# A recurrent attention and mixture-of-experts kernel: the first two units' gate sums spread by one-hot products

## The chip, the cores and the metric

The kernel runs on one core of one Trainium2 chip. The metric is the device time of one execution in microseconds. The core's engines are named as in the profile: PE (TensorE, PEld its weight loads), DVE (VectorE), ACT (ScalarE), POOL (GpSimd) and SP (SyncE, which here only issues DMAs).

## The reference

Two layers follow each other. The first is a gated linear recurrence over 768 time steps for 4 batches of 8 heads with 40 columns each. Its log-space gates are stabilised by a running maximum:

```
m_new = max(f[t] + m, i[t]);  fs = exp(f[t] + m - m_new);  is = exp(i[t] - m_new)
C = fs*C + is * outer(v[t], k[t]);   n = fs*n + is*k[t]
y[t] = sigmoid(o[t]) * (C @ q[t]) / max(|n . q[t]|, 1)
```

The second takes the 3072 rows of 320 columns, picks two of eight experts for each by noisy logits, and adds the two weighted expert outputs, relu(x @ w1[e]) @ w2[e] with 1024 hidden columns.

## The kernel before

The recurrence is worked off in chunks of 64 steps. A *unit* is one chunk of two batches (16 heads, kept as two halves p of 8 heads), and there are 24 units: two pairs of batches by 12 chunks. The state of a pair goes from chunk to chunk inside the buffer of keys and values.

For unit u the steps are: `s_part` (line 326), products of keys and queries on PE into PSUM; `e_part` (305), one matmul for each half that puts the logarithm of the decay matrix into PSUM, and ACT's exponential of it into W; `k_part` (340), DVE scales the keys by W's last column (kd); `p_part` (346), DVE multiplies scores and W; `c_part` (355), PE builds the new state (st) and ACT copies it into the next unit's buffer; `o_part` (368), PE's output products; `f_part` (374), DVE normalises them (dn, tm) and POOL multiplies by the sigmoid gate SG, which gives the row tile XR; `keep_rows` (386) stores XR to memory from POOL's queue; `t_part` (393), PE transposes XR for the router's logits.

The matmul of `e_part` multiplies LE by RE. LE holds, for two units at a time, an identity in rows 0 to 63, the sums a(t) of each head (high and low halves, 32 rows) in rows 64 to 95, and ones in rows 96 and 97. RE holds the causal mask in rows 0 to 63, a one-hot choice of the head in rows 64 to 95, and in rows 96 and 97 the sums g(t) of all heads side by side. There are two LE and two RE, used in turn by pairs of units. Their fixed parts are written by `operands` (223) and `heads` (230).

`gate_math` (189) makes both sums for 128 time steps of all heads on DVE: eight operations, of which the first (192) needs the gate data `fit` and the last (211) writes HL, in 64 rows (head and half) by time. `gate_move` (216) then carries 128 columns of HL to LE and RE with two DMAs, since the sums of 32 rows have to stand side by side in two rows. The first two moves are issued from SP, the third from POOL between units 0 and 1, the others from POOL at even units.

Before the loop, in the order of the program: the gate data of 128 steps, the constants `cet`, keys and queries of unit 0 in four DMAs (rows 0 to 31 and 32 to 39 of each half), an identity, gate data of steps 128 to 383, values of unit 0 (lines 173 to 183); rows that the loads don't fill are written with zeros by `blank` (169) on DVE and POOL. ACT fills LE[0], issues unit 1's four key loads, and fills RE[0] (245 to 252). DVE does the gate math of steps 0 to 127, then that of 128 to 255 (260). `keys` (239) writes zeros and identities into the value buffers on POOL. `gate_steps(4)` (269) does half of the third gate math; its other half, and the rest, are spread over the loop (829, 854). PE warms up with products of zeros (`warm`, 681), 16 of them, does the scores of unit 0, 12 more, and then unit 0's `e_part` (686 to 694).

The loop (785) does for each i, in this order on each engine's own queue: loads of unit i+3, `keep_rows(i-1)`, `k_part` and `p_part` of unit i+1, `c_part` and `o_part` of unit i, the first half of `e_part(i+2)`, `f_part(i)`, gate steps, `t_part(i-1)`, `s_part(i+2)`, the second half of `e_part(i+2)`. Every engine and every DMA queue works in the program's order. DMAs of SP and ACT use eight completion semaphores in turn, so that a DMA waits for the eighth before it to have landed. W, p and kd have two buffers, the output products' PSUM tile one.

From unit 6 on the first expert's weights are loaded and split, from unit 7 on tokens are routed; after the loop the experts are worked off. None of this is touched.

Of the kernel before, what the change touches and what calls it, by code (L numbers as in the profile page):

```python
# [18 lines left out]
L = 64  # L19
# [21 lines left out]
WARM, WARM2 = 16, 12  # L41
# [13 lines left out]
E_H, E_L, E_P, E_SG, E_END = 64, 72, 264, 266, 268  # L55
# [6 lines left out]
def build(ctx, tc, qk, vk, fi, noise, wgn, w1, w2, cst, ce, out):  # L62
# [84 lines left out]
    def load_unit(u, what="kv", q=None):  # L147
        pr, c = divmod(u, NCH)
        if "k" in what:
            for n in (slice(0, 32), slice(32, D)):  # L150
                for p in range(2):
                    (q or SP).dma_start(QK[u % 4][64 * p + n.start:64 * p + n.stop], qk[pr, c, p, n])
        if "v" in what:
            flat = VKS[u % 4].rearrange("p x c -> p (x c)")
            SP.dma_start(flat[0:64, 0:VW], vk[pr, c, 0])
            SP.dma_start(flat[64:128, 648:648 + VW], vk[pr, c, 1])
# [4 lines left out]
    cet = raw[0:KE, 2 * S:2 * S + E_END]  # L161
# [7 lines left out]
    def blank(i, q):  # L169
        q.memset(QK[i][32:64], 0.0)  # L170
        q.memset(QK[i][96:128], 0.0)

    SP.dma_start(fit[:, :, 0:128], fi[:, :, 0:128])
    SP.dma_start(cet, ce)
    V.memset(mt[:, 0:1], -1e30)
    blank(0, V)
    blank(1, P)
    V.memset(rmt[:, 0:256], 1.0)
    V.memset(rmt[:, 0:256].rearrange("p (c t) -> p c t", t=L)[:, :, 0], 0.0)
    load_unit(0, "k")  # L180
    SP.dma_start(cs[:, 0:128], cst[:, 0:128])
    SP.dma_start(fit[:, :, 128:384], fi[:, :, 128:384])
    load_unit(0, "v")

# [31 lines left out]
    def gate_move(kk, q=(SP, SP)):  # L216
        pr, k = divmod(kk, GB)
        j = kk % 2
        src = HL[32 * pr:32 * pr + 32, :, k * GC * L:(k + 1) * GC * L].bitcast(F32)
        q[0].dma_start(LE[j][64:96, :, 64:128].bitcast(F32), src[:, 0].rearrange("r (c t) -> r c t", c=GC))  # L220
        q[1].dma_start(RE[j][96:98].bitcast(F32), src[:, 1])

    def operands(j, p, eng=None):
        if p is None:
            A.activation(LE[j][0:KE], cet[0:KE, None, E_L:E_L + 192].to_broadcast([KE, GC, 192]), AF.Copy)
        else:
            A.activation(RE[j][0:64, p].rearrange("r h (c t) -> r h c t", c=GC),
                         cet[0:64, None, None, 0:L].to_broadcast([64, H, GC, L]), AF.Copy)

    def heads(j, p, eng):  # L230
        o, i = RE[j][64:96, p], cet[64:96, E_H:E_H + H, None].to_broadcast([32, H, GC * L])
        x = cet[64:96, E_P + p:E_P + p + 1]
        if eng is A:
            A.activation(o, i, AF.Copy, scale=x)
        else:
            V.tensor_scalar(o, i, x, None, op0=OP.mult)
# [8 lines left out]
    operands(0, None, A)  # L245
    load_unit(1, "k", A)
    run(gate_math(0, GC * L))
    gate_move(0)
    operands(0, 0, A)
    operands(0, 1, A)  # L250
    heads(0, 0, A)
    heads(0, 1, A)
    load_unit(1, "v")
    blank(2, P)
    for i in range(2):
        keys(i)
    load_unit(2, "k")
    operands(1, None, A)
    operands(1, 0, A)
    run(gate_math(GC * L, 256))  # L260
    gate_move(1)
    heads(1, 0, V)
# [6 lines left out]
    gate_steps(4)  # L269
    blank(3, P)  # L270
    for i in range(2, 4):
        keys(i)
    load_unit(2, "v")
    load_unit(3, "k")
    SP.dma_start(fit[:, :, 384:], fi[:, :, 384:])
# [29 lines left out]
    def e_part(u, ps_=(0, 1), first=False):  # L305
        pr, c = divmod(u, NCH)
        j = (GB * pr + c // GC) % 2
        c = c % GC
        for p in ps_:
            ps = XTB if first and p else psum.tile([128, 512], F32, name="e")  # L310
            T.matmul(ps, LE[j][0:KE, c, 64 - 64 * p:192 - 64 * p], RE[j][0:KE, p, :, c * L:c * L + L], start=True, stop=True)  # L311
            if p == 0:
                W[u] = wk.tile([128, 2, H, L], F32, name="w", bufs=LEAD)
            A.activation(W[u][:, p].rearrange("p h t -> p (h t)"), ps, AF.Exp)
# [31 lines left out]
    def p_part(u):  # L346
        PP[u] = wk.tile([128, 2, H, L], F32, name="p")
        if whole(u):
            V.tensor_mul(PP[u], SQ[u], W[u])
        else:  # L350
            for p in range(2):
                n = half[p]
                V.tensor_mul(PP[u][n, p], SQ[u][n, p], W[u][n, p])
# [20 lines left out]
    def f_part(u, step):  # L374
# [8 lines left out]
        V.scalar_tensor_tensor(tm, dn[:, :, None].to_broadcast([128, H, D]), 1.0, ps[:, :, 0:D], op0=OP.min, op1=OP.mult)  # L383
        P.tensor_mul(XR[u], tm.rearrange("p h d -> p (h d)"), SG[u % 4])  # L384
# [306 lines left out]
    e_part(0, first=True)  # L691
    s_part(1)
    heads(1, 1, A)
    e_part(1, first=True)
    operands(1, 1, A)
    k_part(0)
    p_part(0)
# [86 lines left out]
    i = 0  # L784
    while i < NU - LEAD:
# [42 lines left out]
        f_part(i, lambda: fill(0.15, False))  # L828
        if i < 2:
            gate_steps(4)  # L830
        if i == 0:
            gate_move(2, (P, P))
# [429 lines left out]
def consts():  # L1262
# [16 lines left out]
    e = np.zeros((KE, E_END), np.float32)  # L1279
# [3 lines left out]
    e[96:98, E_L:E_L + 192] = 1  # L1283
# [7 lines left out]
    return c, e  # L1291


def layout(i):
# [27 lines left out]
    c, e = consts()  # L1322
    return dict(qk=qk, vk=vk, fi=fi, noise=nz, wgn=wgn, w1=w1, w2=w2, cst=c, ce=e)
# [20 lines left out]
```

## Time and profile before

| what | us |
|---|---|
| median of 3 runs (526.47 to 527.35) | 526.8 |
| the profiled execution's own time | 524.22 |
| its span, from the first to the last instruction | 522.0 |
| PE busy | 499.3 |
| DVE busy | 339.4 |
| ACT busy | 248.3 |
| POOL busy | 235.7 |

The span is what the views of the trace cover; 2.2 us of the execution lie around it. Times in the trace count from the start of the span. A busy engine is not one at its peak: PE's records overlap. The chain of waits follows the work that ended last back to its start, and names at each step what released it. Its pieces marked "issue" are time in which an engine waited for nothing that the profile shows.

### The profile page before, as it was taken

How to read it: one execution, taken by the hardware profiler on the slowest of the kernel's cores; microseconds unless marked ns; L12 is line 12 of the kernel's file. 1: busy time of each engine (PE TensorE's matmuls, PEld its weight loads, DVE VectorE, ACT ScalarE, POOL GpSimd, SP SyncE). 2: the span in 40 equal slices, each digit the busy share in tenths (PEclk: the TensorE clock that was granted, in tenths of full speed). 3: DMA queues.
4: the chain of work that ended last, by engine and by line, in shares of the span. 5: the costliest groups of instructions: out<-in, count | busy, mean ns of one | idle time of the engine just before them, and what ended most of it. 6: DMA issues, size and time to landing. Idle time of an engine off the chain costs nothing.

```text
span 522.0 us, 13295 instructions
## 1 busy us (share of the span) xinstructions
PE 499.3 (96%) x5129; PEld 469.8 (90%) x5130; DVE 339.4 (65%) x913; ACT 248.3 (48%) x594; POOL 235.7 (45%) x313
## 2 busy tenths in 40 slices
PE   7899989999999899999999999999999999999993
PEld 3788878878989788999999999999999999999993
DVE  7999997986978376763765485367548357555310
ACT  5978978868532255432533354054325315515300
POOL 7545776863324836045415623460562254151033
PEclk9999999999999899999999999999999999999998
DMA  5899999885766627068229515832951583272033
GB/s 155 194 252 240 243 257 237 231 203 199 238 200 213 135 36 222 1 126 264 79 46 274 115 29 128 240 91 46 253 105 52 113 248 88 62 167 26 2 40 40
DMA packets 39737, 76.87 MB, mean 147 GB/s; under 512 B 10389, under 2 KB 29532, under 8 KB 37876
## 3 DMA queue, kind: packets, MB, share of 16 engines
q1 hardware_dynamic: 27636, 52.19, 35.4%
q0 software_dynamic: 11616, 20.57, 20.5%
q10 hardware_dynamic: 416, 3.21, 1.7%
q8 instruction: 42, 0.69, 0.6%
q14 instruction: 27, 0.22, 0.1%
HBM read 52.42 MB, written 17.40 MB: 134 GB/s over the span
## 4 chain that ended last, share of the span: by engine, by line
PE 63%; DVE 13%; DMA 12%; issue 5%; ACT 4%; POOL 2%; SPq 0%; POOLq 0%; DVEq 0%; ACTq 0%
PE s L973 14%; DMA y_out<-y,tok 9%; PE e L973 8%; PE st L1001 4%; PE st L1000 4%; PE o L1001 4%; PE st L999 4%; PE o L1000 4%; PE o L999 4%; PE o L372 3%; PE e L311 2%; DVE hlo L985 2%; PE st L363 2%; PE s L335 2%; PE xt L415 2%
## 5 line engine op out<-in xcount | busy, mean ns | idle before, releaser
L1027 POOL DMA_INDIRECT y_out<-y,tok x53 | 86.9, 1640 | 188.0 <-DVE y L1017 184.9
L984 ACT ACTIVATE hh<-s 128x384 fp32r<-128x384 f32 (+3 forms) x91 | 42.6, 470 | 82.8 <-PE s L973 78.8
L973 PE MATMUL s<-xh,w1h 128*128 128x384 f32 (+6 forms) x273 | 76.5, 335 | 0.0
L743 POOL DMA_INDIRECT xg<-rows,tok x53 | 57.3, 1082 | 29.0 <-issue 15.9
L985 DVE SCALAR_TENSOR_TENSOR hlo<-s,hh 128x384 fp32r<-128x384 f32 (+3 forms) x91 | 47.5, 523 | 22.3 <-ACT hh L984 19.5
L973 PE MATMUL s<-xh,w1l 128*128 128x384 f32 (+6 forms) x273 | 61.7, 334 | 0.0
L1001 PE MATMUL o<-w2h,hlo 128*128 128x320 f32 x184 | 56.9, 309 | 0.7 <-DVE hlo L985 0.7
L1000 PE MATMUL o<-w2l,hh 128*128 128x320 f32 x184 | 56.8, 309 | 0.0
L999 PE MATMUL o<-w2h,hh 128*128 128x320 f32 x184 | 56.3, 306 | 0.2 <-ACT hh L984 0.2
L1001 PE MATMUL st<-w2h,hlo 128*128 128x320 f32 x168 | 52.5, 312 | 0.0
L1000 PE MATMUL st<-w2l,hh 128*128 128x320 f32 x168 | 52.5, 312 | 0.0
L999 PE MATMUL st<-w2h,hh 128*128 128x320 f32 x168 | 51.9, 309 | 0.0
L973 PEld LDWEIGHTS s<-xh,w1h 128*128 128x128 f32 x273 | 49.2, 188 | 1.1
L973 PEld LDWEIGHTS s<-xh,w1l 128*128 128x128 f32 x273 | 47.7, 188 | 1.1 <-DVE xh L777 0.2
L973 PE MATMUL s<-xl,w1h 128*128 128x384 f32 (+6 forms) x182 | 46.0, 334 | 0.0
L984 ACT ACTIVATE hh<-e 128x384 fp32r<-128x384 f32 (+3 forms) x45 | 21.3, 473 | 50.3 <-PE e L973 49.2
L973 PE MATMUL e<-xh,w1h 128*128 128x384 f32 (+6 forms) x135 | 38.8, 341 | 1.1 <-DVE hlo L985 0.6
L1017 DVE TENSOR_SCALAR y<-st,gw 128x320 f32<-128x320 f32 x20 | 11.0, 551 | 43.0 <-PE st L1001 37.1
L1017 DVE TENSOR_SCALAR y<-o,gw 128x320 f32<-128x320 f32 x22 | 12.1, 550 | 39.4 <-PE o L1001 39.3
L384 POOL TENSOR_TENSOR xr<-tm,vk 128x320 f32<-128x320 f32 x24 | 20.9, 873 | 33.9 <-DMA qk<-qk_in 6.8
L1001 PEld LDWEIGHTS o<-w2h,hlo 128*128 128x128 f32 x184 | 34.5, 187 | 0.9 <-DVE hlo L985 0.9
L999 PEld LDWEIGHTS o<-w2h,hh 128*128 128x128 f32 x184 | 34.5, 188 | 0.7 <-ACT hh L984 0.5
(236 smaller groups left out, 1271.8 us busy)
## 6 DMA issues: line engine op xcount, KB each, us to landing
vk<-vk_in SPq DMA_DIRECT2D x48, 242.0 KB
raw<-w_in SPq DMA_DIRECT2D x6, 1536.0 KB
raw<-w_in SPq DMA_DIRECT2D x6, 1280.0 KB
qk<-qk_in SPq DMA_DIRECT2D x46, 128.0 KB
y_out<-zrow SPq DMA_DIRECT2D x15, 320.0 KB
rows<-xr POOLq DMA_DIRECT2D x23, 160.0 KB
xt__2799<-xb SPq DMA_DIRECT2D x40, 72.0 KB
xt__2799<-xb SPq DMA_DIRECT2D x40, 48.0 KB
```

Source lines behind the costliest of these rows:

```text
L311: T.matmul(ps, LE[j][0:KE, c, 64 - 64 * p:192 - 64 * p], RE[j][0:KE, p, :, c * L:c * L + L], start=True, stop=True)
L372: T.matmul(OQ[u][half[p], h, :], PP[u][n, p, h, :], VK[u % 4][p][n, h * 41:h * 41 + 41], start=True, stop=True)
L384: P.tensor_mul(XR[u], tm.rearrange("p h d -> p (h d)"), SG[u % 4])
L743: P.indirect_dma_start(out=XG[0:rows_of(e, t), t], out_offset=None, in_=XD[0:n], in_offset=bass.IndirectOffsetOnAxis(ap=token(e, t), axis= ...
L973: T.matmul(ps[:, 0:n], l, r, start=i == 0, stop=i == len(ops) - 1)
L984: A.activation(hi, x, AF.Relu)
L985: V.scalar_tensor_tensor(lo, x, 0.0, hi.bitcast(F32), op0=OP.max, op1=OP.subtract)
L999: T.matmul(ps, HH[:, j, c], W2H[:, j], start=j == 0, stop=False)
L1000: T.matmul(ps, HH[:, j, c], W2L[:, j], start=False, stop=False)
L1001: T.matmul(ps, HLO[:, j, c], W2H[:, j], start=False, stop=j == 7)
L1017: V.tensor_scalar(y[0:n], ps[0:n], GW[e][0:n, t:t + 1], None, op0=OP.mult)
L1027: st = P.indirect_dma_start(out=out, out_offset=bass.IndirectOffsetOnAxis(ap=token(e, t), axis=0), in_=y[0:n], in_offset=None, compute_op= ...
```

## The change

For units 0 and 1 the sums g no longer go to RE by DMA. RE[0] gets 32 rows (96 to 127) in place of two, LE[0] ones in rows 96 to 127, and `spread` multiplies the 32 rows of HL, repeated over the heads, by a one-hot table: on DVE for unit 0, on POOL for unit 1. The matmul of `e_part` for these units goes over 128 rows. The sums a of the first three pairs of units go into LE by a copy on DVE; g of the second and third pair still by DMA. The gate math of the first 256 steps is done at once, with 256 steps of gate data in the first load, and the rest of the gate data is loaded later, behind unit 2's keys. Units 0 and 1 load keys in two DMAs of 40 rows; unit 1's are issued from SP. The blanks of units 0 and 1 are on POOL, those of unit 2 on DVE and ACT. The one-hot choice of heads in RE[1] is loaded by a DMA of POOL from a new input, `hd` (32 rows of 2048 numbers). Fewer warming products are made. `p_part(0)` is done half by half around `k_part(0)`; the first half of the third gate math stands before the loop, its second half, the third move and `keys(3)` inside `f_part(0)`, between tm and POOL's product XR.

```diff
-WARM, WARM2 = 16, 12
+WARM, WARM2 = 11, 6
...
-            for n in (slice(0, 32), slice(32, D)):
+            for n in (slice(0, 32), slice(32, D)) if u > 1 else (slice(0, D),):
...
-    cet = raw[0:KE, 2 * S:2 * S + E_END]
+    cet = raw[:, 2 * S:2 * S + E_END]
...
-    SP.dma_start(fit[:, :, 0:128], fi[:, :, 0:128])
+    SP.dma_start(fit[:, :, 0:256], fi[:, :, 0:256])
     SP.dma_start(cet, ce)
     V.memset(mt[:, 0:1], -1e30)
-    blank(0, V)
-    blank(1, P)
+    for i in range(2):
+        blank(i, P)
+    A.activation(QK[2][96:128], wz[96:128, None, None, 0:L].to_broadcast([32, 2, H, L]), AF.Copy)
     V.memset(rmt[:, 0:256], 1.0)
     V.memset(rmt[:, 0:256].rearrange("p (c t) -> p c t", t=L)[:, :, 0], 0.0)
+    V.memset(QK[2][32:64], 0.0)
     load_unit(0, "k")
     SP.dma_start(cs[:, 0:128], cst[:, 0:128])
-    SP.dma_start(fit[:, :, 128:384], fi[:, :, 128:384])
     load_unit(0, "v")
+    load_unit(1)
...
-        q[0].dma_start(LE[j][64:96, :, 64:128].bitcast(F32), src[:, 0].rearrange("r (c t) -> r c t", c=GC))
-        q[1].dma_start(RE[j][96:98].bitcast(F32), src[:, 1])
+        le = LE[j][64:96, :, 64:128], src[:, 0].rearrange("r (c t) -> r c t", c=GC)
+        if kk < 3:
+            V.tensor_copy(*le)
+        else:
+            q[0].dma_start(le[0].bitcast(F32), le[1])
+        if kk:
+            q[1].dma_start(RE[j][96:98].bitcast(F32), src[:, 1])
+
+    def spread(c, p, q):
+        t = slice(c * L, c * L + L)
+        q.tensor_mul(RE[0][96:128, p, :, t], HL[0:32, None, 1, t].bitcast(F32).to_broadcast([32, H, L]),
+                     cet[0:32, E_Q + 8 * p:E_Q + 8 * p + H, None].to_broadcast([32, H, L]))
...
+        if p is None:
+            P.dma_start(RE[j][64:96], hd.bitcast(FR))
+            return
...
-    operands(0, None, A)
-    load_unit(1, "k", A)
-    run(gate_math(0, GC * L))
+    heads(1)
+    keys(0)
+    operands(0)
+    for c in range(GC):
+        for p in range(2):
+            operands(0, p, slice(c, c + 1))
+            heads(0, p, slice(c, c + 1))
+        if not c:
+            operands(1)
+    run(gate_math(0, 256))
     gate_move(0)
-    operands(0, 0, A)
-    operands(0, 1, A)
-    heads(0, 0, A)
-    heads(0, 1, A)
-    load_unit(1, "v")
-    blank(2, P)
-    for i in range(2):
-        keys(i)
+    for p in range(2):
+        spread(0, p, V)
+    for p in range(2):
+        spread(1, p, P)
+    gate_move(1)
     load_unit(2, "k")
-    operands(1, None, A)
-    operands(1, 0, A)
-    run(gate_math(GC * L, 256))
-    gate_move(1)
-    heads(1, 0, V)
+    SP.dma_start(fit[:, :, 256:], fi[:, :, 256:])
+    keys(1)
...
-    gate_steps(4)
     blank(3, P)
-    for i in range(2, 4):
-        keys(i)
+    keys(2)
     load_unit(2, "v")
     load_unit(3, "k")
-    SP.dma_start(fit[:, :, 384:], fi[:, :, 384:])
...
-            T.matmul(ps, LE[j][0:KE, c, 64 - 64 * p:192 - 64 * p], RE[j][0:KE, p, :, c * L:c * L + L], start=True, stop=True)
+            n = KE if u >= GC else 128
+            T.matmul(ps, LE[j][0:n, c, 64 - 64 * p:192 - 64 * p], RE[j][0:n, p, :, c * L:c * L + L], start=True, stop=True)
...
-    def f_part(u, step):
+    def f_part(u, step, then=lambda: None):
...
         V.scalar_tensor_tensor(tm, dn[:, :, None].to_broadcast([128, H, D]), 1.0, ps[:, :, 0:D], op0=OP.min, op1=OP.mult)
+        then()
         P.tensor_mul(XR[u], tm.rearrange("p h d -> p (h d)"), SG[u % 4])
...
     e_part(0, first=True)
+    p_part(0, (0,))
+    k_part(0)
+    p_part(0, (1,))
     s_part(1)
-    heads(1, 1, A)
     e_part(1, first=True)
-    operands(1, 1, A)
-    k_part(0)
-    p_part(0)
+    for p in range(2):
+        operands(1, p)
+    gate_steps(4)
...
+    def second():
+        gate_steps(4)
+        gate_move(2, (P, P))
+        keys(3)
...
-        f_part(i, lambda: fill(0.15, False))
-        if i < 2:
+        if i:
+            f_part(i, lambda: fill(0.15, False))
+        else:
+            f_part(0, lambda: None, second)
+        if i == 1:
             gate_steps(4)
-        if i == 0:
-            gate_move(2, (P, P))
```

## Rows read from the trace of the kernel before

**Rows 1.** Chain of waits, 0 to 80 us: start us, us, what

```profile
0.74 0.70 SPq L173
...
1.50 2.51 DMA raw<-ce_in
...
9.10 3.22 DMA re<-hl
...
12.45 0.48 PE e L311
12.95 1.09 ACT w L314 x2
...
21.34 0.81 DVE kd L343
...
29.93 0.50 DVE tm L383
...
30.57 1.13 PE o L372 x32
...
51.65 0.39 PE xt L395 x3
```

**Rows 2.** Timeline of DVE: start us, us, line, operation, shapes [idle before <-releaser]

```profile
2.59 0.91 DVE L171 MEMSET qk<- 32x1024 f32 x1 [0.27 <-issue]
...
3.92 0.47 DVE L192 TENSOR_TENSOR_SCAN xg<-raw,xg 64x128 f32<-64x128 f32 x1
...
5.53 0.26 DVE L204 TENSOR_TENSOR xg<-raw,xg 64x128 f32<-64x128 f32 x1
...
6.46 0.48 DVE L211 SCALAR_TENSOR_TENSOR hl<-hl,raw,xg 64x256 fp32r<-64x256 f32 x1
8.34 0.48 DVE L192 TENSOR_TENSOR_SCAN xg<-raw,xg 64x128 f32<-64x128 f32 x1 [1.41 <-DMA raw<-fi_in]
...
15.18 1.40 DVE L353 TENSOR_TENSOR p<-s,w 64x512 f32<-64x512 f32 x2
16.61 0.83 DVE L343 TENSOR_TENSOR kd<-vk,w 128x640 f32<-128x640 f32 x1
17.47 1.23 DVE L349 TENSOR_TENSOR p<-s,w 128x1024 f32<-128x1024 f32 x1
...
20.40 1.02 DVE L211 SCALAR_TENSOR_TENSOR hl<-hl,raw,xg 64x256 fp32r<-64x256 f32 x1
```

**Rows 3.** Timeline of POOL

```profile
4.73 0.36 POOL L240 MEMSET vk<- 32x328 f32 x1
...
7.02 0.45 POOL L242 COPY vk<-cs 40x320 f32<-40x320 f32 x1 [1.53 <-DMA cs<-cst_in]
...
20.28 0.86 POOL L384 TENSOR_TENSOR xr<-tm,vk 128x320 f32<-128x320 f32 x1 [3.38 <-ACT vk L321]
...
22.94 0.69 POOL L221 DMA_DIRECT2D re<-hl  x1
```

**Rows 4.** Timeline of PE

```profile
21.67 0.49 PE L395 MATMUL xt<-cs,xr 128*128 128x128 f32 x3
...
23.50 0.50 PE L311 MATMUL e<-re,le 98*128 98x512 f32 x1 [0.25 <-ACT w L314]
...
26.66 0.47 PE L311 MATMUL e<-re,le 98*128 98x512 f32 x1 [0.98 <-ACT vk L366]
...
30.57 1.13 PE L372 MATMUL o<-vk,p 104*64 104x41 f32 x32 [0.21 <-DVE tm L383]
```

**Rows 5.** Timeline of SP, whose instructions issue DMAs

```profile
4.57 0.56 SPq L182 DMA_DIRECT2D raw<-fi_in  x1
...
9.10 0.75 SPq L221 DMA_DIRECT2D re<-hl  x1
...
11.12 1.80 SPq L152 DMA_DIRECT2D qk<-qk_in  x4
```

**Rows 6.** POOL's groups by shape: count | busy us, mean ns | idle before

```profile
L144 POOL TENSOR_TENSOR w1l<-raw,w1h 64x512 fp32r<-64x512 f32 x2 | 2.6, 1278 | 0.2
```

More of the change, by code (lines that the diff above doesn't have):

```diff
@@ L54 @@
 KE = 98
-E_H, E_L, E_P, E_SG, E_END = 64, 72, 264, 266, 268
+E_Q, E_H, E_L, E_P, E_SG, E_END = 64, 80, 88, 280, 282, 284
 W1LD, W1AT, W2AT = 6, 8, 21
@@ L61, in build @@
 @with_exitstack
-def build(ctx, tc, qk, vk, fi, noise, wgn, w1, w2, cst, ce, out):
+def build(ctx, tc, qk, vk, fi, noise, wgn, w1, w2, cst, ce, hd, out):
     nc = tc.nc
@@ L219, in gate_move, with operands, heads @@
         src = HL[32 * pr:32 * pr + 32, :, k * GC * L:(k + 1) * GC * L].bitcast(F32)
-        q[0].dma_start(LE[j][64:96, :, 64:128].bitcast(F32), src[:, 0].rearrange("r (c t) -> r c t", c=GC))
-        q[1].dma_start(RE[j][96:98].bitcast(F32), src[:, 1])
-    def operands(j, p, eng=None):
+        le = LE[j][64:96, :, 64:128], src[:, 0].rearrange("r (c t) -> r c t", c=GC)
[9 more added lines that the diff above has]
+                     cet[0:32, E_Q + 8 * p:E_Q + 8 * p + H, None].to_broadcast([32, H, L]))
+    def operands(j, p=None, cc=slice(0, GC)):
+        n = cc.stop - cc.start
         if p is None:
-            A.activation(LE[j][0:KE], cet[0:KE, None, E_L:E_L + 192].to_broadcast([KE, GC, 192]), AF.Copy)
-        else:
[L227 to L236, printed above, removed]
+            m = KE if j else 128
+            A.activation(LE[j][0:m], cet[0:m, None, E_L:E_L + 192].to_broadcast([m, GC, 192]), AF.Copy)
+        else:
+            A.activation(RE[j][0:64, p].rearrange("r h (c t) -> r h c t", c=GC)[:, :, cc],
+                         cet[0:64, None, None, 0:L].to_broadcast([64, H, n, L]), AF.Copy)
+    def heads(j, p=None, cc=slice(0, GC)):
+        if p is None:
+            P.dma_start(RE[j][64:96], hd.bitcast(FR))
+            return
+        t = slice(cc.start * L, cc.stop * L)
+        A.activation(RE[j][64:96, p, :, t], cet[64:96, E_H:E_H + H, None].to_broadcast([32, H, t.stop - t.start]), AF.Copy,
+                     scale=cet[64:96, E_P + p:E_P + p + 1])
     def keys(i):
@@ L344, in k_part, with p_part @@
                          W[u][:, :, :, L - 1:L].to_broadcast([128, 2, H, D]))
-    def p_part(u):
-        PP[u] = wk.tile([128, 2, H, L], F32, name="p")
+    def p_part(u, ps_=(0, 1)):
+        if 0 in ps_:
+            PP[u] = wk.tile([128, 2, H, L], F32, name="p")
         if whole(u):
@@ L350, in p_part @@
         else:
-            for p in range(2):
+            for p in ps_:
                 n = half[p]
@@ L1277, in consts @@
     c[:, C_COL:C_COL + NE * TC] = (32 * (np.arange(NE * TC) // TC) + np.arange(NE * TC) % TC)[None]
-    e = np.zeros((KE, E_END), np.float32)
+    e = np.zeros((128, E_END), np.float32)
     t = np.arange(64)
@@ L1282, in consts @@
     e[0:64, E_L + 64:E_L + 128] = np.eye(64)
-    e[96:98, E_L:E_L + 192] = 1
+    e[96:128, E_L:E_L + 192] = 1
+    one = np.concatenate([np.eye(16), np.eye(16)]).astype(np.float32)
+    e[0:32, E_Q:E_Q + 16] = one
+    hd = np.ascontiguousarray(np.repeat(one, GC * L, 1)).reshape(32, 2, H, GC * L)
     e[0:64, E_SG] = -(np.arange(64) // 16 % 2)
@@ L1290, in consts @@
                 e[r + h, E_H + h] = 1
-    return c, e
+    return c, e, hd
 def layout(i):
@@ L1321, in layout @@
     w1, w2 = np.ascontiguousarray(w1), np.ascontiguousarray(w2)
-    c, e = consts()
-    return dict(qk=qk, vk=vk, fi=fi, noise=nz, wgn=wgn, w1=w1, w2=w2, cst=c, ce=e)
+    c, e, hd = consts()
+    return dict(qk=qk, vk=vk, fi=fi, noise=nz, wgn=wgn, w1=w1, w2=w2, cst=c, ce=e, hd=hd)
 OUT_ROWS = NTOK + BLK
```

## The prediction

> **What bounds the kernel now.** Of the profiled execution's span of 522.0 us I read the chain of waits of the first 80 us first, because the change touches nothing behind the first few units. The reader sees three stretches there [rows 1]. Up to 12.45 the first gate product waits on moves: gate data and constants, a load, then the move of the gate sums into RE (issued at 9.10, 3.22 us). From 21.34 to 29.93 every piece of the chain is DVE's. From 30.57, unit 3's output products, to 51.65 it is PE's almost without a gap. So a shift of the head is worth what is left of it at 30.57, and I follow the change to that point.
>
> The timeline of DVE shows that it is the head's second limit [rows 2]: gate math from 3.92 to 6.94 (128 columns), the second gate math from 8.34 behind a wait of 1.41 us for gate data, and kd of unit 1 at 16.61. Call that start K; 4.27 us after it (20.40 + 0.48 undisturbed) the third set of gate sums is written. The last update took 1.02 us where an earlier one of its shape took 0.48: POOL's product XR of unit 0 ran from 20.28 to 21.14 [rows 3].
>
> The timeline of PE gives the other limit [rows 4]. It transposes XR of unit 0 at 21.67, and from there to unit 3's output products it idles 0.25, 0.98 and 0.21 us: 1.44 us of slack. If XR comes later than that allows, PE is late at 30.57 whatever DVE does.
>
> **The change, step by step.**
>
> *First loads and gate math.* Twice the columns of gate data come in the first load. It is issued at 0.74; the constants behind it flew 2.51 us [rows 1], so it lands near 3.25. DVE loses two blank writes of 0.91 us and gets one [rows 2], so it is free by then: the scan starts 0.65 us earlier. One pass of 256 columns replaces two of 128. From the 640 and 1024 element products (0.83 and 1.23 us) an element costs 1.04 ns over 0.16 us fixed; a scan (0.47 at 128) 2.4 ns. So 128 more columns add two scans at 0.31, five short operations at 0.13 and the last update at 0.27: 1.5 us. The sums are ready at 3.25 + 3.02 + 1.5 = 7.8 (bounds: no added cost 6.3, double cost 9.3), against 6.94 for the first half before.
>
> *Products in place of the move.* The 3.22 us go, and with them SP's issue of 0.75 [rows 5]. DVE makes a 128-column copy into LE (0.25) and two products of 32x512; each costs about 0.70, the half of the 64x512 pair (1.40) [rows 2]. POOL makes two; its nearest row is 1.28 us for a 64x512 product [rows 6] (bounds: 0.86, the 320-element XR [rows 3], to twice 1.28, because both inputs are repeated, for which there is no row). Alone, DVE would be done at 9.45. But they start together, and rows 2 and 3 show an update on DVE finishing only after POOL's product. Taking turns, DVE's first ends at 8.75, POOL's at 10.0, DVE's second at 10.7, POOL's second at 12.0; the copy for units 2 and 3 follows, to 12.25. The Trainium skill (SBUF — State Buffer, section "Who interferes with whom") states a rule against this split: an instruction of DVE with two SBUF inputs and one of GpSimd that reads SBUF hold one port in turn, each for its whole length. The single collision in rows 2 and 3 agrees; no row has two such trains. By the rule K below is 16.1 and the sum 0.3 us larger; without it DVE would be free at 9.7 and the sum stands.
>
> The first gate product goes from 12.45 to about 8.8, the second follows at 10.75, and the exponentials (0.48 + 1.09 behind it [rows 1]) end at 12.3. DVE then does half of p (0.70), kd (0.83), the other half (0.70): 14.5 with turns, about 12.1 without.
>
> *The rest of the gate data.* Before K, DVE now has four steps of the third gate math, 1.6 us (3.92 to 5.53 undisturbed). They need columns 256 up, loaded on SP behind the move for units 2 and 3, which waits for the sums (7.8), and behind unit 2's key loads: 7.9 + 0.75 + 1.80 = 10.45 [rows 5]. The nearest such load took 3.77 us, from 4.57 [rows 5] to the scan that waited for it at 8.34 [rows 2], so it lands at 14.2; bounds 2.51 [rows 1] and twice that, so 12.95 to 15.5. Either way K is 14.2 + 1.6 = 15.8 or 14.5 + 1.6 = 16.1. I take 15.8, whose last wait has a row of its own kind: 0.8 us earlier than 16.61. Of the 3.6 us at the first product, 0.8 reach DVE.
>
> *What is moved past POOL.* XR of unit 0 now stands on POOL behind the move of the third gate sums (issue 0.69), which waits for DVE to write them, and behind keys(3): two writes of 0.36 and two copies of 0.45 [rows 3], 1.7 us with their gaps. The sums are written at 15.8 + 4.3 = 20.1; XR ends at 20.1 + 0.1 + 0.69 + 1.7 + 0.1 + 0.86 = 23.55, where it ended at 21.14. Allowing 0.25 for the weight load, PE's transposes start at 23.8: 2.13 us after 21.67. Less the slack of 1.44, PE reaches unit 3's output products 0.7 us late. DVE by itself would be 0.6 us early there (0.8 less a copy of 0.2), so PE decides. Sum: +0.7 us. Behind XR on POOL stand the row store and XR of unit 1, behind SP's unit 4 value load its whole queue; those are used two units later.
>
> *Costed at nothing.* Eleven fewer warming products: PE waits for the gate product anyway; if that came by 8 us they would count. ACT loses four load issues, gets a blank of QK[2] and splits RE's fills by chunk; its last fill ends near 10, before POOL's products. POOL's two blanks, one-hot load and keys(0) end before 7.8. Unit 0's and 1's loads in 40 rows end by about 9. Gate products over 128 rows instead of 98 have the same columns. Unit 0's LE and RE moves by DMA that go were on no path except the first.
>
> **Forecast.** The profiled run's own time is 524.22, a span of 522.0; it would read 524.9. The median of the runs is 526.8; the sum goes on that: **527.5 us**. A measurement tells some 0.2% from no change, 1.05 us here, so this is no change.
>
> **Rivals.**
>
> *A: DVE alone decides (faster).* If XR's lateness is absorbed on PE, the shift at 30.57 is that of K and one copy of 0.2. With no turns and the early landing K is 12.95 + 1.6 = 14.55, so 2.05 - 0.2 = 1.85 us are gained: 524.9. For it speaks that the chain before names DVE and never XR in this stretch; against it that PE works in order and the transposes stand ahead of unit 3's scores.
>
> *B: both half way.* K of 14.55, but XR still decides: it ends at 22.3, PE is 0.9 late against 1.44 of slack, so 0.55 is gained: 526.2, still no change.
>
> *C: the rest of the gate data lands late (slower).* It sits behind the loads of four units on the same queue. At 15.5, K is 17.1, XR ends at 24.85 and the end moves by 2.0: 528.8. It decides from a landing of 14.6 on, where the sum passes 1.05. For it speaks the 3.77 us; against it that the issue is only at 10.45.
>
> *D: the one-hot products save nothing.* If the 256-column math took double (9.3), the first product would still come at 10.3, so the move's removal is visible in any case; the price lies within C.
>
> **Chances.** Forecast 0.45, B 0.12, A 0.21, C 0.20, D 0.02. Faster by over 0.2%: 0.21 (A). Within: 0.57 (forecast and B). Slower: 0.22 (C and D). The range holds all from A to C, 524.9 to 528.8; the likeliest case alone spans 526.6 to 527.9.
>
> **What would show it.** Right: first gate product at 8.5 to 9.2; DVE and POOL products stretched or in turns until 12; a wait of DVE for gate data, or none with its scan near 14.3; kd of unit 1 at 15.5 to 16.3; XR of unit 0 ending at 23 to 24 and PE waiting for it. Wrong: kd of unit 1 before 15, XR before 22.5, or PE idle for something other than XR between 18 and 30. Units 4 on should look the same, moved by one constant.

## The result and the profile after

The changed kernel takes 532.64 us (median of 5 runs, 532.18 to 534.48) against 526.8 (5 runs, 524.43 to 530.97): a ratio of 1.0122 with a 95% interval of 1.008 to 1.0163. Ratios and their intervals, here and below, compare fast executions alone, so a ratio is not the quotient of the two medians. The change is slower, outside the range of the prediction. The profiled execution took 532.64 us, with a span of 530.5 against 522.0.

The chain of waits of the changed kernel, 0 to 80 us, answers to [rows 1] (columns: start us, us, what).

```profile
18.84 0.79 DVE kd L356
...
23.83 0.71 POOL re L228
26.39 0.83 POOL xr L399
27.27 0.90 PE xt L410 x3
...
41.86 1.22 issue
```

The first move of the gate sums, which stood on the chain before (9.10, 3.22 us), is gone from it. What decides now is kd of unit 1 and behind it the order on POOL (the third move, keys(3), XR of unit 0). PE follows at 27.27, where the transposes stood at 21.67 before [rows 4].

The timeline of DVE, which answers to [rows 2]:

```profile
3.68 0.74 DVE L194 TENSOR_TENSOR_SCAN xg<-raw,xg 64x256 f32<-64x256 f32 x1 [0.99 <-DMA raw<-fi_in]
...
7.42 0.82 DVE L213 SCALAR_TENSOR_TENSOR hl<-hl,raw,xg 64x512 fp32r<-64x512 f32 x1
8.34 0.29 DVE L224 CAST le<-hl 32x128 fp32r<-32x128 f32 x1
8.65 2.13 DVE L232 TENSOR_TENSOR re<-hl,raw 32x512 fp32r<-32x512 f32 x2
...
13.31 0.70 DVE L367 TENSOR_TENSOR p<-s,w 64x512 f32<-64x512 f32 x1
17.28 0.48 DVE L194 TENSOR_TENSOR_SCAN xg<-raw,xg 64x128 f32<-64x128 f32 x1 [3.28 <-DMA raw<-fi_in]
...
18.84 0.79 DVE L356 TENSOR_TENSOR kd<-vk,w 128x640 f32<-128x640 f32 x1
...
22.59 0.47 DVE L213 SCALAR_TENSOR_TENSOR hl<-hl,raw,xg 64x256 fp32r<-64x256 f32 x1
```

The gate sums are ready at 8.24 and go to LE and RE without a DMA. DVE is done with unit 0 at 14.0 and then stands for 3.28 us, waiting for the rest of the gate data. So kd of unit 1 starts at 18.84, not at 16.61 as before [rows 2].

POOL and PE, which answer to [rows 3] and [rows 4]:

```profile
8.65 3.03 POOL L232 TENSOR_TENSOR re<-hl,raw 32x512 fp32r<-32x512 f32 x2
...
23.83 0.71 POOL L228 DMA_DIRECT2D re<-hl  x1 [5.05 <-PE e L324]
...
25.94 0.45 POOL L257 COPY vk<-cs 64x320 f32<-64x320 f32 x1
26.36 0.85 POOL L399 TENSOR_TENSOR xr<-tm,vk 128x320 f32<-128x320 f32 x1
```

```profile
10.61 0.58 PE L324 MATMUL e<-re,le 128*128 128x512 f32 x1
...
27.27 0.90 PE L410 MATMUL xt<-cs,xr 128*128 128x128 f32 x3 [3.83 <-POOL xr L399]
...
36.03 1.19 PE L386 MATMUL o<-vk,p 128*64 128x41 f32 x24
```

The first gate product moved from 12.45 to 10.61, a gain of 1.84 us; unit 3's output products moved from 30.57 to 36.03, a loss of 5.46. The 5.05 us of POOL's wait are put down to a PE product that ended at 23.43; the move also waits for DVE's sums, written at 22.59 + 0.47 = 23.06, and 0.77 us passed between them and its issue.

The timeline of SP, which answers to [rows 5], and SP's waits from 3 to 22 us (columns: who waited <- for what: us, times, longest):

```profile
4.64 0.92 SPq L152 DMA_DIRECT2D qk<-qk_in  x2
...
8.26 0.79 SPq L228 DMA_DIRECT2D re<-hl  x1
9.10 2.59 SPq L152 DMA_DIRECT2D qk<-qk_in  x4
12.41 0.59 SPq L276 DMA_DIRECT2D raw<-fi_in  x1
```

```profile
SPq L276 <- DMA qk<-qk_in: 0.7, 1, 0.7
```

The load of the rest of the gate data is issued at 12.41, after a wait of 0.72 us for a key load. DMAs of one queue share eight completion semaphores, and the eighth issue before this one is unit 1's second key load (issued by 5.56). By the trace's semaphores that load was complete at 12.39.

Why a load issued by 5.6 needs until 12.39 shows in the windows of both kernels (columns: window, us, busy us of PE, PEld, DVE, ACT, POOL with instructions, granted clock of PE, busy share of the 16 DMA engines, GB/s). Before:

```profile
4.00:8.00 4.00, 4.00 (x43) 2.07 (x42) 2.67 (x10) 2.46 (x3) 2.29 (x5) 1.00 0.56 161
8.00:12.00 4.00, 2.49 (x11) 0.98 (x10) 3.42 (x9) 3.72 (x5) 3.70 (x6) 1.00 0.71 170
```

After:

```profile
4.00:8.00 4.00, 3.38 (x30) 1.80 (x30) 3.74 (x9) 3.91 (x7) 2.81 (x6) 1.00 0.94 245
8.00:12.00 4.00, 3.43 (x21) 1.58 (x18) 3.75 (x6) 3.07 (x6) 3.85 (x4) 1.00 1.00 213
...
20.00:24.00 4.00, 2.20 (x63) 1.74 (x60) 3.76 (x10) 3.19 (x7) 0.17 (x1) 1.00 0.79 183
24.00:28.00 4.00, 0.73 (x3) 0.50 (x3) 3.86 (x8) 0.07 (x1) 3.48 (x7) 0.51 0.02 4
28.00:32.00 4.00, 4.00 (x94) 3.35 (x93) 3.30 (x7) 2.71 (x6) 1.94 (x4) 0.63 0.88 218
```

From 4 to 12 us the DMA engines had room before (0.56 and 0.71) and have none after (0.94 and 1.00). Later, from 24 to 28, nearly nothing moves: PE works 0.73 of 4 us, and the DMA queues stand still too, as SP's next load (unit 4's values, at 27.24) waits for the same XR. In the windows of the transposes and of unit 3's scores PE is granted 0.51 and 0.63 of full speed, so it runs for most of them at the lower of its two levels, 1.2 of 2.4 GHz. It had worked 2.20 of 4 us in the window before.

### The profile page after: what moved, and what is told of

Its sections match the earlier page's. It is cut to its first block, busy times and chain, and to the rows that moved or that the text cites. A ratio compares the mean times of both kernels' runs of the same rounds, so it can differ in the third digit from the quotient of the medians.

```text
span 530.5 us, 13267 instructions
## 1 busy us (share of the span) xinstructions
PE 502.8 (95%) x5119; PEld 472.2 (89%) x5119; DVE 340.1 (64%) x908; ACT 249.6 (47%) x598; POOL 239.8 (45%) x315
## 4 chain that ended last, share of the span: by engine, by line
PE 65%; DMA 13%; DVE 9%; issue 4%; POOL 4%; ACT 3%; SPq 1%; POOLq 0%; DVEq 0%; ACTq 0%
PE s L997 14%; DMA y_out<-y,tok 9%; PE e L997 7%; PE o L386 4%; PE st L1025 4%; PE st L1024 4%; PE o L1025 4%; PE st L1023 4%; PE o L1024 4%; PE o L1023 4%; PE e L324 3%; PE s L348 3%; PE st L377 3%; DVE hlo L1009 2%; PE xt L430 2%
## 5 line engine op out<-in xcount | busy, mean ns | idle before, releaser
L760 POOL DMA_INDIRECT xg<-rows,tok x53 | 57.5, 1084 | 28.9 <-issue 16.1
```

Of the source, the lines that this page charges most:

```text
L760: P.indirect_dma_start(out=XG[0:rows_of(e, t), t], out_offset=None, in_=XD[0:n], in_offset=bass.IndirectOffsetOnAxis(ap=token(e, t), axis= ...
```

## The experiments

The theory after the first look had two parts. *Late data*: the DMA engines and SP's queue are full in the head, and the rest of the gate data lands late. *POOL's order*: XR of unit 0 stands behind the third move and keys(3). The rival was a *cold PE*: fewer warming products make the time. Ratios are to runs of the kernel before on the same chip.

### 1. The rest of the gate data loaded first

```diff
     load_unit(0, "v")
+    SP.dma_start(fit[:, :, 256:], fi[:, :, 256:])
     load_unit(1)
...
     load_unit(2, "k")
-    SP.dma_start(fit[:, :, 256:], fi[:, :, 256:])
```

> The changed kernel with one move: the gate data of steps 256 up is loaded behind unit 0's values, ahead of unit 1's loads. Late-data theory (the loss starts where DVE waits 3.28 us for this load, and comes to PE through XR of unit 0): the load is issued at 4.6 and lands by 9; DVE's scan follows p of unit 0 at 14.1 without a wait, kd of unit 1 starts at 15.7 (18.84 in the changed kernel), XR of unit 0 ends at 24.0 (27.2), unit 3's output products start at 31.7 (36.0) and the time falls by 4 to 6 us, to 527 to 529. POOL-order theory (XR behind the third move and keys(3) is the loss by itself): PE still waits over 2 us for XR; the time falls by 3 at most. Cold-PE theory (fewer warming products let the clock fall): the clock still falls at 24 and 45 us and the time falls by less than 3 us.

Measured: 529.92 us (10 runs), ratio 1.0061 [1.0019, 1.0103]. DVE's timeline, and the waits from 8 to 20 us:

```profile
14.07 0.48 DVE L195 TENSOR_TENSOR_SCAN xg<-raw,xg 64x128 f32<-64x128 f32 x1
...
18.73 0.83 DVE L356 TENSOR_TENSOR kd<-vk,w 128x640 f32<-128x640 f32 x1 [3.10 <-POOL anew L490]
```

```profile
PE s L345 <- DMA qk<-qk_in: 3.3, 1, 3.3
```

DVE's wait for gate data is gone and kd of unit 1 starts at the same time all the same. The profile names POOL, which had been done; PE shows the cause: it stands 3.3 us for unit 1's keys, so unit 1's scores, gate product and exponential are late. What went first made the next load late: the gate data came in time and the keys did not. Part of the rest is PE's clock, which was granted at 0.55 and 0.59 of full speed from 12 to 20 us in this profile. From the start of unit 1's scores to kd it takes 3.92 us here (14.81 to 18.73), and 2.80 in the seventh and eleventh kernels, where PE runs at full speed in that stretch; so some 1.1 us of kd's lateness is the clock's. XR starts at 26.29 as before the edit. What the edit did gain shows on PE:

```profile
27.19 0.55 PE L410 MATMUL xt<-cs,xr 128*128 128x128 f32 x3 [2.44 <-POOL xr L399]
...
34.42 0.58 PE L386 MATMUL o<-vk,p 128*64 128x41 f32 x13
```

The transposes start where they did (27.27), and take 0.55 in place of 0.90; unit 3's output products come at 34.42 in place of 36.03. PE stood still earlier here, and its half-speed stretch lies earlier: from 12 to 20 us, as said, with a full clock from 20 to 36. So of the loss at unit 3, some 1.6 us was the price of the clock after XR. This profile's gain is that, and not an earlier kd. The interval overlaps that of the changed kernel (1.008 to 1.0163), so this edit by itself is not shown to gain in the time.

### 2. XR ahead of the third move and keys(3)

```diff
-        then()
         P.tensor_mul(XR[u], tm.rearrange("p h d -> p (h d)"), SG[u % 4])
+        then()
```

> The changed kernel with one move: POOL's product XR of unit 0 stands ahead of the second half of the third gate math, the third move and keys(3). Late-data theory: DVE still waits 3.3 us for the gate data and kd of unit 1 stays at 18.8; XR ends at 22.7 instead of 27.2, so PE's wait of 3.83 us goes; unit 3's output products start at 33.4 as DVE then decides; the time falls by 2.5 to 4 us, to 528.5 to 530. POOL-order theory: the whole loss goes, to 527 or less. Cold-PE theory: no change within 1 us.

Measured: 528.11 us (10 runs), ratio 1.006 [1.0026, 1.0094]. The DVE wait for gate data stays, 3.46 us, with kd of unit 1 at 19.54. POOL's and PE's timelines:

```profile
22.56 0.86 POOL L398 TENSOR_TENSOR xr<-tm,vk 128x320 f32<-128x320 f32 x1 [4.92 <-ACT vk L380]
25.17 0.72 POOL L228 DMA_DIRECT2D re<-hl  x1 [1.75 <-DVE le L224]
```

```profile
25.03 0.84 PE L410 MATMUL xt<-cs,xr 128*128 128x128 f32 x3
```

XR goes from 26.36 to 22.56 and the transposes from 27.27 to 25.03, still 3.4 us later than before. XR had ended at 23.42; PE was then still at earlier products, at half speed (granted 0.58 and 0.57 from 20 to 28 us). Unit 3's output products come at 34.29, after 0.70 us of waiting for DVE, so DVE decides there, as was expected (33.4 was said). The ratio is that of the first edit, here by an earlier XR; this interval, too, overlaps that of the changed kernel.

### 3. Both

> Both moves at once. Late-data theory: kd of unit 1 at 15.7, XR of unit 0 at 19.5 to 20.5, unit 3's output products at 30.1 to 30.6 as in the kernel before, and the time is that of before within 1 us (525.5 to 527.5). POOL-order theory: the same as with XR moved alone. Cold-PE theory: still over 530.

Measured: 526.66 us (10 runs), ratio 1.0032 [0.9996, 1.0067]. Together the edits take back 0.9 of the 1.2%, with an interval below that of the changed kernel: that is shown. Whether they add up (0.6% each) can't be told within the noise. What is left of the wait is this (DVE, PE, ACT):

```profile
18.21 0.83 DVE L356 TENSOR_TENSOR kd<-vk,w 128x640 f32<-128x640 f32 x1 [2.48 <-DMA vk<-vk_in]
```

```profile
14.29 0.69 PE L345 MATMUL s<-qk,cs 64*64 64x256 f32 x2 [2.70 <-POOL vk L258]
```

```profile
17.53 0.59 ACT L327 ACTIVATE w<-xt 128x512 f32<-128x512 f32 x1
```

The profile puts kd's wait down to unit 1's values, but by the trace's semaphores these had landed by 16.34, when SP's next load on the same semaphore was issued. Kd follows ACT's exponential, which ends at 18.12 and follows the scores. These began at 14.29, after PE had stood 2.70 us. The POOL copy that is named there writes the value buffer, which the scores don't read; unit 1's second key load was complete by 14.22, when SP's next load on its semaphore was issued. Then the scores ran at half speed (granted 0.64 and 0.51 from 12 to 20 us): from scores to kd it is 3.92 us again. So what is left is unit 1's keys and the clock.

### 4. Unit 0's and 1's keys in 32 and 8 rows again

```diff
-            for n in (slice(0, 32), slice(32, D)) if u > 1 else (slice(0, D),):
+            for n in (slice(0, 32), slice(32, D)):
```

> The changed kernel with the keys of units 0 and 1 loaded in pieces of 32 and 8 rows again. If the 40-row loads, which spread over fewer DMA engines, are what makes unit 1's keys land at 12 and hold the gate data's issue to 12.41: issue at 11.7 or earlier, landing at 15.5 to 16, kd of unit 1 at 17.3, the time falls by 1.5 to 2.5 us. If the queue is only full: no change within 1 us, landing at 17.

Measured: 532.15 us (4 runs), ratio 1.0135 [1.0073, 1.0197]. The scan of the third gate math starts at 17.46 after a wait of 3.13 us. The shape of the key loads is not the cause. The load of the gate data was issued at 11.89 here, 0.52 us sooner than in the changed kernel, and its scan starts 0.18 us later (17.46 for 17.28). In a stretch where the DMA engines are full, an earlier issue alone brought the data no sooner. This profile has PE at half speed from 20 to 40 us, in an execution of 532.76 us:

```profile
36.00:40.00 4.00, 4.00 (x73) 3.11 (x74) 1.12 (x4) 2.46 (x6) 0.60 (x2) 0.50 0.81 209
```

### 5. No head pattern from memory

```diff
-    heads(1)
...
+    heads(1, 0)
     run(gate_math(0, 256))
...
     e_part(0, first=True)
+    heads(1, 1)
```

> The changed kernel without the 256 KB load of the head pattern: ScalarE writes the same rows instead, one half before the first exponentials and one behind them (about 1.05 us each, by its 32x1024 write at the start). In the changed kernel the 16 DMA engines are busy for 0.94 and 1.00 of the stretches 4 to 8 and 8 to 12 us, against 0.56 and 0.71 before. Theory of bytes (the head pattern takes the engines while unit 1's keys and values and the rest of the gate data stand behind it): the share falls by about a quarter of 4 us in 8 to 12, unit 1's keys are there about 1.2 us sooner (11.2 in place of 12.4), the rest of the gate data lands near 16, kd of unit 1 starts near 17.6, and the time falls by 1 to 2 us to 530.6 to 531.6, as POOL's order still holds the first row product. Rival (order alone: what is issued before the rest of the gate data sets its landing, the pattern runs beside it): landing 17.0 to 17.3 again, 532.6. Rival (ScalarE becomes the bound): the first exponential starts later than 11.4 and the time is 533 or more.

Measured: 532.19 us (12 runs), ratio 1.0116 [1.008, 1.0153]. The window from 8 to 12 us and DVE's timeline:

```profile
8.00:12.00 4.00, 2.74 (x22) 1.17 (x21) 3.82 (x6) 3.94 (x7) 3.85 (x4) 1.00 0.89 200
```

```profile
16.49 0.48 DVE L194 TENSOR_TENSOR_SCAN xg<-raw,xg 64x128 f32<-64x128 f32 x1 [2.42 <-DMA raw<-fi_in]
...
18.31 0.79 DVE L356 TENSOR_TENSOR kd<-vk,w 128x640 f32<-128x640 f32 x1
```

The trace moves as the theory of bytes says, by less than it said: the share falls from 1.00 to 0.89, unit 1's second key load is complete at 11.68 in place of 12.39, the gate data load is issued at 11.70, and kd of unit 1 starts 0.53 us sooner. In the time this can't be told from nothing. The Trainium skill says that loads started by different engines run on the same 16 DMA engines and interleave (DMA: Bandwidth & Descriptors, section "Issuing engines are not separate DMA queues"). The trace agrees: a load from POOL's queue delayed one of SP's by 0.7 us.

### 6. All one-hot products on VectorE

```diff
-        spread(1, p, P)
+        spread(1, p, V)
```

> The changed kernel with all four one-hot products on VectorE, none on POOL. Theory of the shared lock (the two engines took turns: 2.13 us for VectorE's two, 3.03 for POOL's two, both from 8.65): alone, VectorE's product takes what its other 64x512 product takes, 0.7 us, so the four end by 11.5, POOL's keys(1) starts at 8.7 and the second copy into LE takes 0.29 us again in place of 0.95. Rival (no turns, the two shapes simply cost 1.06 and 1.5): the four take 4.3 us and end at 12.9, and the first p product moves from 11.86 to 13.2. For the time: neither lies on the path that sets kd of unit 1, which waits for the rest of the gate data, so 531.9 to 533.0 under the first, up to 533.8 under the second.

Measured: 533.57 us (4 runs), ratio 1.0164 [1.0092, 1.0236]. DVE's and POOL's timelines:

```profile
8.57 3.00 DVE L232 TENSOR_TENSOR re<-hl,raw 32x512 fp32r<-32x512 f32 x4
11.60 0.51 DVE L224 CAST le<-hl 32x128 fp32r<-32x128 f32 x1
```

```profile
8.53 0.36 POOL L254 MEMSET vk<- 32x328 f32 x1
...
9.38 0.80 POOL L256 COPY vk<-cs 40x320 f32<-40x320 f32 x1
```

DVE does four products in the time in which it and POOL did two each (8.65 to 11.68). Singly, in the trace of the changed kernel, the four end at 9.33 (DVE), 10.23 (POOL), 10.78 (DVE) and 11.68 (POOL), one behind the other. That is the taking of turns which the prediction cited from the Trainium skill (SBUF — State Buffer, section "Who interferes with whom"), and the trace agrees: here the first two products, beside POOL's writes of zeros, take 0.68 each, and the last two, beside POOL's copies, 0.93. The split over two engines gained nothing. It didn't set the time either: the scan waits 4.02 us for the gate data and kd of unit 1 starts at 19.79. The median lies above the range that was expected, which its interval takes in.

### 7 and 8. Both edits, no head pattern, and then the old warming products

The seventh kernel is the third with the edit of the fifth; the eighth adds this:

```diff
-WARM, WARM2 = 11, 6
+WARM, WARM2 = 16, 12
```

> The third kernel (rest of the gate data before unit 1's loads, first row product ahead of the third move and keys(3)) and the head pattern written by ScalarE. There kd of unit 1 stood at 18.21 and waited for its values. Theory of bytes: these land about 1.2 us sooner, kd of unit 1 starts near 17.0, later units stand 1 us nearer to the kernel before (+2.4 becomes about +1.2 at unit 3), time 525.0 to 526.2 where the third kernel had 526.66. Rival (order alone): kd near 18.2, 526.2 to 527.2. Rival (a cold TensorE decides): the clock falls again after 13 us whatever lands, and the time stays within 0.5 us of the third kernel's.

> The kernel of the run before this one with the kernel before's 28 warming products in place of 17. Theory of a cold TensorE: the first full grant comes at 6 us or sooner and the half-speed stretch after 13 us goes or shortens by half; the score and state products of units 1 and 2 take half as long there and the time falls by 1 us or more against that run. Theory of bytes: the warming products fill a stretch in which nothing on TensorE is late; the second set stands ahead of the first gate product on the in-order queue and makes it later by up to 1.5 us (12.1 in place of 10.6), which unit 1's values hide; time within 0.7 us of the run before.

Measured: the seventh 525.9 us (12 runs), ratio 1.0011 [0.998, 1.0042]; the eighth 524.18 us (12 runs), ratio 0.996 [0.9928, 0.9993]. Kd of unit 1 in the seventh and in the eighth:

```profile
16.11 0.83 DVE L356 TENSOR_TENSOR kd<-vk,w 128x640 f32<-128x640 f32 x1 [0.25 <-ACT w L327]
```

```profile
15.96 0.83 DVE L356 TENSOR_TENSOR kd<-vk,w 128x640 f32<-128x640 f32 x1
```

K is 16.1 where it was 18.21 in the third kernel, and 15.96 is what the prediction had for the change itself. Of the 2.1 us some 1.0 is the loads: without the pattern unit 1's scores begin at 13.31 and 13.03 in place of 14.29. The other 1.1 is the clock, which is full there in the seventh's profile. PE's transposes stand at 21.98 and 21.82, next to the 21.67 of before [rows 4]. The medians of the seventh and the eighth are 1.7 us apart, and the intervals overlap by little, so the times alone don't show what the warming products bring. The two profiles don't either: unit 3's output products stand at 31.00 and 30.84, and it is the eighth that has a half-speed stretch in the head (0.79 and 0.78 from 12 to 20 us).

What does show is the granted clock of every execution over its whole span, which the results list. In the mean it is 0.984 in the seventh and 0.990 in the eighth, a difference of 0.0058 with a standard error of 0.0017. Over all the executions that the ratios use, within one kernel, 0.01 of that clock goes with some 2.9 us of time (correlation -0.70). The 0.0058 would thus go with 1.7 us. That the two go together is measured; that the one makes the other is not, as no run sets the clock by itself.

### 9 and 10. The warming products alone

The ninth is the changed kernel with 16 and 12 warming products, the tenth the kernel before with 11 and 6.

> The changed kernel with the kernel before's 28 warming products in place of 17, nothing else. Theory of a cold TensorE by itself: the half-speed stretch at 24 to 31 us goes and the time falls by 1.5 us or more, to 531 or less. Theory of bytes and POOL's order: that stretch follows from TensorE's wait for the first row product (3.83 us before the transposes at 27.27), which warming products in the first 11 us do not shorten; the first row product stays at 26 to 27 and the time within 0.8 us of 532.6.

> The kernel before with the changed kernel's 17 warming products in place of 28, nothing else: the price of the removed products without the rest of the change. If they cost nothing, as the prediction had it: 525.4 to 526.6 beside 525.9, the first gate product still at 12.4 as it waits for the move. If the pair of runs before (525.90 with 17, 524.18 with 28) shows the price of a cold TensorE: 1 to 2.5 us slower, with a half-speed stretch somewhere in the first 50 us that the kernel before does not have.

Measured: the ninth 531.62 us (6 runs), ratio 1.0115 [1.0062, 1.0167], where the changed kernel has 1.0122; the tenth 526.07 us (12 runs), ratio 0.9993 [0.9948, 1.0037]. By themselves the eleven products cost nothing that can be measured in the time, in either kernel, so a cold PE is not the cause of the loss. Yet the tenth's profile has a half-speed stretch in the head that the profile of the kernel before doesn't have there:

```profile
12.00:16.00 4.00, 4.00 (x51) 2.79 (x53) 3.85 (x8) 2.84 (x5) 3.66 (x7) 0.57 0.82 193
16.00:20.00 4.00, 3.99 (x73) 3.33 (x73) 3.84 (x8) 2.63 (x5) 1.07 (x8) 0.50 0.74 194
```

Its span is 524.1 us against 522.0. One profiled execution tells what the clock did in that execution; the two medians don't follow it. The clock over the whole span is lower in the mean of the tenth's executions, too: 0.983 against 0.987 before (standard error of the difference 0.0014). In the changed kernel the products bring nothing there: 0.979, and 0.978 in the ninth.

### 11. Both edits and the old warming products, head pattern loaded

> The third kernel (rest of the gate data before unit 1's loads, first row product ahead of the third move and keys(3)) with 28 warming products, the 256 KB head pattern still loaded. Against the eighth kernel (524.18) it differs by that load alone. Theory of bytes: kd of unit 1 stands at 18 as in the third kernel against 16 in the eighth, and the time is 0.7 to 1.8 us above the eighth's. Rival (warm TensorE alone decides): 523.7 to 524.7. Rival (the head pattern alone decides): 526 to 527, as in the third.

Measured: 525.17 us (12 runs), ratio 0.9989 [0.9955, 1.0024]. Kd of unit 1 starts at 17.08, against 15.96 without the pattern, and against 16.11 in the seventh kernel, where PE runs at full speed from unit 1's scores to kd as it does here. So the 256 KB of the pattern are worth 0.97 us of K. The third kernel's scores began at the same time (14.29 and 14.28), and its kd at 18.21: that difference is the clock's. For the time the pattern has three pairs: 1.0122 and 1.0116, 1.0032 and 1.0011, 0.9989 and 0.996. All three are lower without it, no one of them beyond its interval.

### 12. A quarter of the rest of the gate data first

The eighth kernel, with columns 256 to 383 ahead of unit 1's loads and the others behind unit 2's values:

```diff
-    SP.dma_start(fit[:, :, 256:], fi[:, :, 256:])
+    SP.dma_start(fit[:, :, 256:384], fi[:, :, 256:384])
     load_unit(1)
...
     load_unit(2, "v")
+    SP.dma_start(fit[:, :, 384:], fi[:, :, 384:])
```

> The eighth kernel with only 128 of the 512 columns of the rest of the gate data ahead of unit 1's loads (64 KB of 256 KB), the others behind unit 2's values. Theory of bytes: 192 KB less stand ahead of unit 1's keys and values, at 205 to 235 GB/s some 0.8 to 0.9 us; its keys land sooner by that, its gate product at 13.3 in place of 14.1, kd of unit 1 at 15.3 to 15.6 in place of 15.96 (the scan's last step at 15.40 holds it), and the time is 0 to 0.8 us under the eighth's. Rival (another wait holds units 2 and 3, as kd of unit 2 waits for its values at 21.24): the first products move and the time stays within 0.3 us.

Measured: 522.92 us (12 runs), ratio 0.9956 [0.9925, 0.9987]. DVE's and PE's timelines:

```profile
15.77 0.79 DVE L357 TENSOR_TENSOR kd<-vk,w 128x640 f32<-128x640 f32 x1
```

```profile
13.44 0.50 PE L325 MATMUL e<-re,le 128*128 128x512 f32 x1
...
21.01 0.49 PE L411 MATMUL xt<-cs,xr 128*128 128x128 f32 x3
```

Unit 1's gate product is at 13.44 (14.13 in the eighth), the transposes at 21.01. Its median is 1.26 us under the eighth's and its ratio 0.0004 under, so the two can't be told apart; both beat the kernel before and the changed kernel. Its profile has a clock of 0.997 over the span and no half-speed stretch between the first 5 us and the last 4. At unit 3's output products it is only 0.41 us ahead of the kernel before (30.16 for 30.57), so most of the 0.44% lies further on. No view here shows that part. Over all executions the clock is 0.992 in the mean, against 0.987 before, and by the 2.9 us for 0.01 this would go with 1.3 us.

## Why the prediction was wrong, step by step

**The first loads and the gate math** came out: scan at 3.68 (3.25 was said), sums ready at 8.24 (7.8). **The products in turns** came out too: the first on DVE ended at 9.33 and the last on POOL at 11.68 (12.0 was said). The first gate product was later than said, 10.61 for 8.8. Its sums and its half of RE were there at 9.33, but PE still had the six warming products in front of it (they started at 8.59), so the gain at the head was 1.84 us and not 3.6. PE was slow there in this execution: unit 0's scores took 1.97 us and the six products 2.37, where the first kernel's profile, with as many warming products, has 1.15 and 1.47 and its first gate product at 9.58. The granted clock reads 1.00 in both, so these rows don't tell why. The wait for the gate data hid the difference. DVE was done with unit 0 at 14.0 (14.5 was said).

**The step that failed is "The rest of the gate data".** Its landing was put at 14.2, with 15.5 as the upper bound, and it was 17.25. The parts of the 3.05 us: the issue was put at 10.45 and came at 12.41. Of these 1.96 us, 0.4 come from the sums, 0.8 from unit 2's key loads (2.59 us of issue for 1.80) and 0.72 from the wait for unit 1's key load. The flight was put at 3.75 and took 4.84. The row it was taken from carries 128 KB and this load 256 KB, and from 12 to 16 us the DMA engines were busy for 0.84 of the time. The semaphores are not the whole of it: unit 1's values, issued by 6.7, were still on their way when SP's loads behind the gate data came to the same semaphores (13.42 and 14.47), and in the fourth kernel an issue 0.52 us sooner brought the data no sooner. In its place the runs showed that the head is now filled by DMA: unit 1's keys went from ACT's eight semaphores to SP's, with a load of 256 KB beside them, and each later load on SP waits for the eighth before it. The sentence "Unit 0's and 1's loads in 40 rows end by about 9", among the items costed at nothing, was the root of it: the keys ended at 12.39. So was "one-hot load ... end before 7.8": its issue ended then, its bytes came until 10.9. The other kernels bear this out. With the gate data ahead and the pattern still loaded, unit 1's scores begin at 14.81, 14.29 and 14.28 (first, third, eleventh); without the pattern's 256 KB they begin at 13.31 and 13.03 (seventh, eighth), and K at a full clock is 16.11 for 17.08. In the fifth, which changes the bytes alone, the scan of the gate data starts at 16.49 for 17.28. The rest of the lateness of K in the first and third, 1.1 us, is the clock's, which the prediction did not price.

**The step on POOL's order** had the right mechanism and chain, as XR did decide PE. K to the sums was 4.22 us (4.3 was said). From the sums to the move's issue 0.77 us passed where 0.1 was said, and the rest was right. With K 3.04 late XR ended at 27.21 for 23.55. The 0.25 us allowed for the weight load of the transposes was 0.06 (27.21 to 27.27). The second kernel moves XR as this step says (26.36 to 22.56); the 0.6% in its ratio is not clear of the changed kernel's interval, and only with the first edit is the gain clear of it.

**The slack on PE** was right too. By the prediction's own arithmetic transposes at 27.19 give 27.19 - 21.67 - 1.44 = 4.1 us at unit 3, and the first kernel, whose PE runs at full speed there, lost 34.42 - 30.57 = 3.9. The changed kernel lost 5.46: a clock that falls while PE waits for XR was in no term of the sum and cost the other 1.6. The clock over the whole span agrees in size: it is 0.979 in the mean of the changed kernel's executions and 0.985 to 0.987 in those of the kernel before, which by 2.9 us for 0.01 goes with some 2 us. That everything from unit 4 on would move by one constant did not hold in this profile: the loss is 5.46 at unit 3, 5.70 at unit 4, 8.40 at unit 5, 8.11 at unit 6 and 8.5 over the span. The chain has 1.22 us of "issue" at 41.86, and another half-speed stretch followed (44.6 to 48.0). Such a wait of 0.94 to 1.50 us between 40.7 and 48.5 stands in the profiles of the first, fifth, sixth and ninth kernels as well, and one of 1.15 at 72.88 in that of the kernel before. Each of these six ends 1.4 to 1.8 us after a 16 KB load on the DMA queue of instructions had ended (at 41.49 and 43.09 in the changed kernel). That would fit a PE that waits for its instructions; no run tests it, and the cause stays open.

**The rivals.** C was the right one, with its size off: it decides from a landing of 14.6 on, as it said, and was priced to a landing of 15.5 only. By its arithmetic, 17.25 gives 526.8 + 3.7 = 530.5; POOL's 0.67 us and the clock's 1.6 make 532.8. That this meets the median of 532.64 is in part luck: the terms are those of one profile up to unit 3, and that profile lost 3 us more behind it, while the medians are only 5.8 us apart. C also spoke of the loads of four units ahead of the gate data; by the diff they are those of three. The bound was the error: twice the flight of one load on a queue with room was no bound for a load on a queue without any. A failed with the landing. **Eleven fewer warming products** cost nothing in the change as it was, as said (ninth and tenth kernels). Once little else is late they may count: from the seventh to the eighth kernel the ratio falls by 0.5%, from the third to the eleventh by 0.4%, both with intervals that overlap, and in both pairs the clock over the span is higher with them (0.984 to 0.990, 0.984 to 0.989). The 0.2% that the forecast called the least that can be told was too fine: these intervals are some 0.3 to 0.4% to either side.

## What to carry to other kernels

Before a load is moved ahead or onto another queue, add up the bytes and the busy share of the DMA engines in that stretch, and count the issues to see whose completion the next load waits for; what is loaded earlier makes something else later, and the bound for a landing has to hold for a full queue. An operation of one engine whose result the main engine waits for should stand ahead of everything on its queue that is needed later: here this and the earlier gate data took back 0.9 of 1.2% together. A change that gains at its own place can still be kept by mending what it pushed back: with a quarter of the gate data loaded early, XR first on POOL, the head pattern made on chip and the old warming products it takes 522.92 us, by its ratio 0.44% less than before (0.13 to 0.75%).

## What the runs showed of the hardware

A key load of 160 KB issued by 5.56 us was complete only at 12.39, 6.8 us later, while the DMA engines were busy for 0.94 and 1.00 of the time. A move issued from POOL starts 0.77 us after the last sum that it waits for (23.06 to 23.83; before the change 0.73, 21.42 to 22.15). Four products on DVE alone take as long as two on DVE and two on POOL together (3.00 and 3.03 us). Where in the head PE's half-speed stretch falls was worth 1.6 us behind XR (unit 3's output products at 36.03 and 34.42 after transposes at the same time) and 1.1 us between unit 1's scores and kd (3.92 us at half speed, 2.80 at full). Half-speed stretches of PE differ between profiles whose times agree: 20 us of them in the head in the fourth kernel's execution of 532.76 us, 10 in that of the changed kernel's of 532.64. Over the span, 0.01 of mean granted clock went with 2.9 us within a kernel, over 195 executions.
